# Attention and two expert layers on one core: new load order at the start, and the first batch's units in five stretches

## The chip, the core and the metric

The program runs on one core of a Trainium2 chip. The time is the device time of one execution in microseconds (us). Five engines with an instruction queue each take part: PE (TensorE, matmuls), DVE (VectorE), ACT (ScalarE), POOL (GpSimd) and SP (SyncE, which here issues DMAs). Every queue runs in order: an instruction that waits holds all that stand behind it.

## What is computed

```python
def _attn_ref(q, k, v, p):                 # q, k, v: [4, 8, 576, 64], p: [4, 8, 32, 64]
    p_packed = sm_attn(p, k, v)            # softmax attention of the 32 pack rows on the 576 keys
    return sm_attn(q, p_packed, p_packed)  # the 576 queries on the 32 packed rows
...
x = attn_out.transpose(0, 2, 1, 3).reshape(2304, 512)
h = x @ w_in;  y = (h * tanh(softplus(h))) @ w_out        # w_in [512, 2048], w_out [2048, 512], "mish"
h = y @ w_in2; out = where(h > 0, h, exp(min(h, 0)) - 1) @ w_out2
```

The weights come as float64 and are read as pairs of 32-bit words.

## The kernel before

**Weights.** A weight tile of 128 rows is loaded raw (`load_raw`, line 127, on SP's queue) and decoded to float32 by `decode`: `s0` on ACT (line 162 in the start-up form `exps=True`, line 164 later), then on DVE `s1` (169), `s2` (177, only without `exps`) and `s3` (182). A tile of w_out (named `w1o0` to `w1o15`, of which `w1o4` holds the rows of unit index 4) is then split into a high and a low part, on ACT (204) and DVE (210). A tile of w_in (`w1i r c`: four row blocks r of each of four column groups c) stays whole; `fold` (line 523) multiplies column group c by the packed rows of a batch and gives `G[b, c]`, split by ACT (204) and DVE (210).

**Units.** The first layer is done in 128 units: batch b, token half e (288 tokens), 128 columns kk of the hidden layer. `gemm1` (563 to 565, 6 matmuls) makes the first product from `G[b, kk // 4]`, `mish` (572 to 574, ACT, ACT, DVE) the activation, and `gemm2` (591 to 593, 12 matmuls), two units later, adds the unit into an accumulator. The accumulators of one token half fill both buffers of `ps_a`: when the units pass to the other half, the next `gemm2` waits until `y` has been copied out (line 275, half on ACT and half on DVE, or added on DVE at 603 where the half has been there before). `order1` gives the order of the units. For batch 0 it is four stretches of eight units: half 0 with kk 0 to 7, half 1 with kk 0 to 7, half 0 with kk 8 to 15, half 1 with kk 8 to 15. So a new column group of w_in is needed at units 0, 4, 16 and 20.

**Order of the rest.** `startup()` writes out by hand the attention of batch 0 and the decode of the first eight weight tiles; its PE, DVE, ACT and SP work stands in that order. `mixture1()` then walks over the units and puts between them, by due times, the decode of the other 24 tiles (`DEC1`), the folds of batch 0 (`F0`), the attention and the folds of batch 1 (`ATT1`, `FOLDOFF`), the reloads of decoded w_in tiles (`RELOFF`) and, from unit 34, the second layer's weights. Tile's scheduler orders what comes from there; where `keep_in_program_order` is called, the instruction keeps its place among those marked like it. ACT needs another function table for the exponentials of an attention than for Mish: each change is an `ACT_TABLE_LOAD`.

**Loads at the start.** On SP: two small parts of p for batch 0, the four k tiles, two raw tiles, q, eight raw tiles. On ACT: two small parts of p, then v. On POOL: the p of the other batches. The DMAs of SP and ACT share eight semaphores, so the ninth waits for the first to land. PE runs `WARM` matmuls on the identity matrix before its first real work.

Of the kernel before, what the change touches and what calls it, by code (L numbers as in the profile page):

```python
# [18 lines left out]
    DEC1=[9, 37],  # L19
    F0=[3, 12, 17],  # L20
# [6 lines left out]
    RELOFF=-5,  # L27
    NU=28,
    EVA='va',
    WARM=16,  # L30
    YL=[12, 13, 14],
# [10 lines left out]
def kernel(  # L42
# [81 lines left out]
    def load_raw(name, r, c):  # L124
# [5 lines left out]
        if name[1] == "2":  # L130
            tc.keep_in_program_order(ins)
# [108 lines left out]
    def load_heads(src, dst, b, g, nm, eng):  # L240
# [9 lines left out]
        elif nm == "k" or b == 0:  # L250

            t = home([128, S // 32, 32], F32, f"{nm}{b}_{g}")
            eng.dma_start(
                out=t.rearrange("p c d -> p (c d)"),
                in_=src[b, 2 * g:2 * g + 2].rearrange("h (t j) d -> (h t) (j d)", t=64),
            )
        else:
# [24 lines left out]
    def transpose_heads(src, dst, b, g, nm):  # L282
        def blocks32():
            o = small([128, 2, HALF], F32, f"{nm}{b}_{g}")
            nc.vector.transpose(
                out=o.rearrange("p e s -> p (e s)"), in_=src.pop((b, g)).rearrange("p c d -> p (c d)")
            )
            dst[b, g] = o

        return [blocks32]  # L290
# [259 lines left out]
    order1 = [(e, h * NK // 2 + i) for h in range(2) for e in range(2) for i in range(NK // 2)]  # L550
# [210 lines left out]
    DEC1 = P["DEC1"]  # L761

    def startup():
        pr = [slot([128, n * H // 2, D], F32, f"pr{n}") for n in (1, B - 1)]
        ps_ = p.rearrange("b (g s) n d -> s n (b g) d", s=2)
        for x, (a, n) in enumerate(((0, H // 2), (H // 2, (B - 1) * H // 2))):
            for s in range(2):
                for th in range(2):
                    r = 64 * s + 32 * th
                    eng = nc.gpsimd if x else (nc.sync, nc.scalar)[s]  # L770
                    eng.dma_start(out=pr[x][r:r + 32], in_=ps_[s][:, a:a + n, :])
# [9 lines left out]
        nc.scalar.preload_act_table_set("exp_and_others")  # L781
# [9 lines left out]
        dec = [decode(*w1dec.popleft(), exps=True) for _ in range(8)]  # L791
# [4 lines left out]
        def turn_p(x):  # L796
# [7 lines left out]
            hk[0][0], hk[1][0], hk[2][0], hk[3][0], sc[0][0], sc[1][0], sc[0][1], sc[1][1], *parts(0, 0), sc[0][2],  # L804
            a1t0[0], a1t0[1], a1t1[0], a1t1[1], *parts(1, 0), pk[0][0], hq[0][0], hq[1][0], sc[1][2], *parts(0, 1, 3, 4),
            pk[1][0], pk[0][1], hq[2][0], hq[3][0], pk[0][2], pk[1][1], *parts(2, 0), *parts(3, 0), *parts(1, 1, 3, 4),
# [160 lines left out]
```

## Time and profile before

| what | value |
|---|---|
| three runs, median (lowest to highest) | 819.1 us (817.96 to 820.22) |
| profiled execution, its span | 817.5 us |
| PE busy | 776.2 us (95%) |
| DVE busy, ACT busy | 439.6 us (54%), 341.2 us (42%) |
| chain that ended last | PE 85%, DVE 7%, DMA 4%, ACT 3% |

No time of the profiled execution itself is given beside its span; the lowest run lies 0.5 us above the span and the median 1.6 us. The page's strip of 40 slices shows PE at nine tenths or more from the eighth slice on, and in the first seven slices (some 143 us) less; there DVE stands at eight to nine tenths in most slices, and the granted PE clock is below full in five of the first six. The granted clock has two levels, 2.4 GHz (1.00) and 1.2 GHz (0.50); a value between is a mean over a stretch.

### The profile page before, as it was taken

How to read it: one execution, taken by the hardware profiler on the slowest of the kernel's cores; microseconds unless marked ns; L12 is line 12 of the kernel's file. 1: busy time of each engine (PE TensorE's matmuls, PEld its weight loads, DVE VectorE, ACT ScalarE, POOL GpSimd, SP SyncE). 2: the span in 40 equal slices, each digit the busy share in tenths (PEclk: the TensorE clock that was granted, in tenths of full speed). 3: DMA queues.
4: the chain of work that ended last, by engine and by line, in shares of the span. 5: the costliest groups of instructions: out<-in, count | busy, mean ns of one | idle time of the engine just before them, and what ended most of it. 6: DMA issues, size and time to landing. Idle time of an engine off the chain costs nothing.

```text
span 817.5 us, 13068 instructions
## 1 busy us (share of the span) xinstructions
PE 776.2 (95%) x5212; PEld 669.6 (82%) x5212; DVE 439.6 (54%) x845; ACT 341.2 (42%) x672; POOL 25.0 (3%) x50
## 2 busy tenths in 40 slices
PE   6468879999999999999999999999999999999997
PEld 5147769889888998999998888888888888888886
DVE  3998886955687448573427743422352334332342
ACT  2347744666475746564434432312231223221322
POOL 1000000000001010000000000000000000000000
PEclk8787979999999999999999999999999999999999
DMA  9962973376656774440682311200030001000000
GB/s 250 411 242 90 326 175 147 124 235 133 215 195 221 191 207 164 150 134 30 227 292 79 102 52 35 68 1 1 1 90 1 1 1 51 14 1 0 35 18 26
DMA packets 67837, 96.80 MB, mean 118 GB/s; under 512 B 34624, under 2 KB 43328, under 8 KB 67776
## 3 DMA queue, kind: packets, MB, share of 16 engines
q1 hardware_dynamic: 61408, 77.02, 29.8%
q0 software_dynamic: 4928, 17.70, 5.5%
q10 hardware_dynamic: 1440, 1.25, 0.7%
q8 instruction: 41, 0.67, 0.3%
q14 instruction: 20, 0.16, 0.1%
HBM read 73.92 MB, written 22.02 MB: 117 GB/s over the span
## 4 chain that ended last, share of the span: by engine, by line
PE 85%; DVE 7%; DMA 4%; ACT 3%; issue 1%; ACTq 0%; SPq 0%; DVEq 0%
PE h L654 8%; PE h L655 8%; PE h L653 8%; PE o L676 8%; PE o L677 8%; PE o L678 8%; PE acc L592 7%; PE acc L591 7%; PE acc L593 7%; PE h L563 4%; PE h L564 4%; PE h L565 4%; PE pm L523 1%; DMA raw_w1o<-in_moe_w_out_dram 1%; DMA v<-in_v_dram 1%
## 5 line engine op out<-in xcount | busy, mean ns | idle before, releaser
L592 PE MATMUL acc<-gl,w1oh 128*128 128x288 f32 x512 | 152.5, 300 | 1.6 <-DVE gl L574 1.4
L593 PE MATMUL acc<-gh,w1ol 128*128 128x288 f32 x512 | 151.7, 299 | 0.0
L591 PE MATMUL acc<-gh,w1oh 128*128 128x288 f32 x512 | 148.9, 298 | 2.6 <-DVE y L275 2.6
L654 PE MATMUL h<-yl,w2ih 128*128 128x512 f32 (+1 forms) x320 | 117.7, 368 | 0.0
L655 PE MATMUL h<-yh,w2il 128*128 128x512 f32 (+1 forms) x320 | 117.5, 368 | 0.0
L653 PE MATMUL h<-yh,w2ih 128*128 128x512 f32 (+1 forms) x320 | 116.6, 368 | 0.0
L676 PE MATMUL o<-w2oh,gh 128*128 128x512 f32 x288 | 112.4, 390 | 1.1 <-ACT ob L273 0.7
L677 PE MATMUL o<-w2ol,gh 128*128 128x512 f32 x288 | 112.2, 390 | 0.0
L657 ACT ACTIVATE t<-h 128x512 f32<-128x512 f32 (+1 forms) x80 | 42.8, 553 | 165.5 <-PE h L655 151.0
L658 DVE TENSOR_SCALAR t<-t 128x512 f32<-128x512 f32 (+1 forms) x80 | 31.7, 399 | 142.5 <-ACT t L657 141.7
L678 PE MATMUL o<-w2oh,gl 128*128 128x512 f32 x288 | 108.3, 389 | 0.0
L592 PEld LDWEIGHTS acc<-gl,w1oh 128*128 128x128 f32 x512 | 97.4, 190 | 9.1 <-DVE gl L574 5.0
L591 PEld LDWEIGHTS acc<-gh,w1oh 128*128 128x128 f32 x512 | 96.3, 191 | 7.4 <-DVE y L275 4.6
L593 PEld LDWEIGHTS acc<-gh,w1ol 128*128 128x128 f32 x512 | 97.2, 190 | 3.9 <-issue 3.6
L574 DVE TENSOR_TENSOR gl<-t,gh 128x288 fp32r<-128x288 f32 x128 | 57.7, 453 | 78.2 <-ACT gh L573 77.6
L563 PE MATMUL h<-a2h,gh 128*128 128x288 f32 x256 | 78.4, 309 | 9.7 <-ACT a2h L204 6.0
L572 ACT ACTIVATE t<-h 128x288 f32<-128x288 f32 x128 | 52.1, 408 | 84.1 <-PE h L565 81.8
L564 PE MATMUL h<-a2l,gh 128*128 128x288 f32 x256 | 77.5, 303 | 3.0 <-DVE a2l L208 3.0
L204 ACT ACTIVATE gh<-t 128x512 fp32r<-128x512 f32 (+1 forms) x80 | 46.6, 588 | 78.6 <-DVE t L659 49.1
L565 PE MATMUL h<-a2h,gl 128*128 128x288 f32 x256 | 76.9, 302 | 0.0
L208 DVE TENSOR_TENSOR gl<-t,gh 128x512 fp32r<-128x512 f32 (+1 forms) x80 | 50.2, 637 | 41.0 <-ACT gh L204 39.5
L653 PEld LDWEIGHTS h<-yh,w2ih 128*128 128x128 f32 x320 | 60.3, 188 | 10.3
(107 smaller groups left out, 1098.7 us busy)
## 6 DMA issues: line engine op xcount, KB each, us to landing
w1r<-w_dr SPq DMA_DIRECT2D x24, 512.0 KB, 6.0
raw_w1i<-in_moe_w_in_dram SPq DMA_DIRECT2D x16, 512.0 KB, 8.9
raw_w1o<-in_moe_w_out_dram SPq DMA_DIRECT2D x16, 512.0 KB, 8.2
raw_w2i<-in_moe_w_in_dram SPq DMA_DIRECT2D x16, 512.0 KB, 4.3
raw_w2o<-in_moe_w_out_dram SPq DMA_DIRECT2D x16, 512.0 KB, 3.8
k<-in_k_dram SPq DMA_DIRECT2D x16, 288.0 KB, 7.2
y_dr<-y POOLq DMA_DIRECT2D x16, 288.0 KB, 3.8
w_dr<-w1v POOLq DMA_DIRECT2D x8, 512.0 KB, 6.1
```

The costliest lines, as they stand in the source:

```text
L563: nc.tensor.matmul(out=hp, lhsT=wh, rhs=xh, start=(kt == 0), stop=False)
L564: nc.tensor.matmul(out=hp, lhsT=wh, rhs=xl, start=False, stop=False)
L565: nc.tensor.matmul(out=hp, lhsT=wl, rhs=xh, start=False, stop=(kt == 1))
L591: nc.tensor.matmul(out=o, lhsT=wh[:, cs], rhs=gh, start=first, stop=False)
L592: nc.tensor.matmul(out=o, lhsT=wh[:, cs], rhs=gl, start=False, stop=False)
L593: nc.tensor.matmul(out=o, lhsT=wl[:, cs], rhs=gh, start=False, stop=last)
L653: nc.tensor.matmul(out=hp, lhsT=wh, rhs=xh, start=(i == 0), stop=False)
L654: nc.tensor.matmul(out=hp, lhsT=wh, rhs=xl, start=False, stop=False)
L655: nc.tensor.matmul(out=hp, lhsT=wl, rhs=xh, start=False, stop=(i == 3))
L676: nc.tensor.matmul(out=o, lhsT=gh[:, ts], rhs=wh, start=(kk == 0), stop=False)
L677: nc.tensor.matmul(out=o, lhsT=gh[:, ts], rhs=wl, start=False, stop=False)
L678: nc.tensor.matmul(out=o, lhsT=gl[:, ts], rhs=wh, start=False, stop=(kk == NK - 1))
```

## The change

At the start, the four k tiles are issued by SP and ACT in turn, v goes from ACT's queue to SP's, behind k; the raw tiles are interleaved with q, and the p of batches 1 to 3 goes from POOL's queue to SP's, behind the first eight raw tiles. `EXPS` = 12 tiles instead of 8 are decoded in `startup()` in its form without `s2`; four of them are column group 1 of w_in. The w1 loads, the k loads of batch 1 and their transposes keep their program order. The units of batch 0 come in five stretches: half 0 with kk 0 to 3, half 1 with 0 to 7, half 0 with 4 to 11, half 1 with 8 to 15, half 0 with 12 to 15. A new column group is needed at units 0, 8, 16 and 24, and the accumulators pass to the other half at units 4, 12, 20, 28 and 32. The due times `F0`, `DEC1` and `RELOFF` move with it, and the y tiles of batch 0 lie in the pool `up`.

```diff
-    DEC1=[9, 37],
-    F0=[3, 12, 17],
+    DEC1=[10, 32],
+    F0=[6, 14, 20],
...
-    RELOFF=-5,
+    RELOFF=(-2, -5),
+    EXPS=12,
...
-        if name[1] == "2":
-            tc.keep_in_program_order(ins)
+        tc.keep_in_program_order(ins)
...
+            if b == 1:
+                tc.keep_in_program_order(ins)
...
-    order1 = [(e, h * NK // 2 + i) for h in range(2) for e in range(2) for i in range(NK // 2)]
+    order1 = [(e, kk) for e, a, n in ((0, 0, 1), (1, 0, 2), (0, 1, 2), (1, 2, 2), (0, 3, 1)) for kk in range(4 * a, 4 * (a + n))]
...
-        first = kk == 0 or (blk < 2 and kk == NK // 2)
-        last = kk == NK - 1 or (blk < 2 and kk == NK // 2 - 1)
+        first = n == 0 or order1[n - 1][0] != blk
+        last = n + 1 == len(order1) or order1[n + 1][0] != blk
...
-                    ysum[blk, d] = small([128, 2, HALF], F32, f"y{blk}_{d}")
+                    ysum[blk, d] = (small if blk > 1 else slot)([128, 2, HALF], F32, f"y{blk}_{d}")
...
+        load_p(0, (nc.sync, nc.scalar))
...
-            load_heads(k, kt_in, 0, g, "k", nc.sync)
-        for kt in range(2):
-            load_vt(0, kt, nc.scalar)
+            load_heads(k, kt_in, 0, g, "k", (nc.sync, nc.scalar)[g % 2])
         nc.scalar.preload_act_table_set("exp_and_others")
-        load_w1(2)
         for kt in range(2):
+            load_vt(0, kt)
+        for kt in range(2):
+            load_w1(1)
             load_kt(q, qt_in, 0, kt, "q")
         load_w1(6)
-        load_w1(LEAD)
+        load_p(1, (nc.sync, nc.sync))
+        load_w1(EXPS - 8 + LEAD)
...
-        dec = [decode(*w1dec.popleft(), exps=True) for _ in range(8)]
+        dec = [decode(*w1dec.popleft(), exps=True) for _ in range(EXPS)]
...
-                at.setdefault(i0 + NK + 4 * c + P['RELOFF'], []).append(lambda c=c: reload_w1i(c))
+                at.setdefault(i0 + NK + 4 * c + P['RELOFF'][b > 1], []).append(lambda c=c: reload_w1i(c))
```

The hand-written list in `startup()` changes too: the first raw tile is decoded after the transposes of the first attention, not before, and `s0` of the four tiles of column group 1 stands at the list's end, ahead of the units.

On ACT, where the units begin (h1 is a unit's first product, t1 its activation; a2h0 belongs to the attention of batch 0; w1oh0 is the high part of w_out's first rows), before:

```order
L162 ACTIVATE raw_w1o3_0_191<-raw_w1o3_0_191 128x512
L204 ACTIVATE a2h0_431<-a2t0_1_445 128x576
L572 ACT_TABLE_LOAD
L572 ACTIVATE t1_489<-h1_482 128x288
L204 ACTIVATE w1oh0_0_199<-dec_201 128x512
```

and now:

```order
L162 ACTIVATE raw_w1o3_0_187<-raw_w1o3_0_187 128x512
L204 ACTIVATE a2h0_441<-a2t0_1_455 128x576
L162 ACTIVATE raw_w1i0_1_193<-raw_w1i0_1_193 128x512
L162 ACTIVATE raw_w1i1_1_195<-raw_w1i1_1_195 128x512
L162 ACTIVATE raw_w1i2_1_197<-raw_w1i2_1_197 128x512
L162 ACTIVATE raw_w1i3_1_199<-raw_w1i3_1_199 128x512
L204 ACTIVATE w1oh0_0_207<-dec_209 128x512
L576 ACT_TABLE_LOAD
L576 ACTIVATE t1_499<-h1_492 128x288
```

The four `s0` of column group 1 and one split now stand ahead of the table load and of the first Mish.

On DVE, from the last decode step of column group 1 (`w1v1_2` from `raw_w1i3_1`, which releases the second fold) to the copies of `y`, now:

```order
L182 SCALAR_TENSOR_TENSOR w1v1_2_216<-raw_w1i3_1_199,w1v1_2_216 128x512
L806 STREAM_TRANSPOSE pT3_98<-pr3_118 128x768
L177 SCALAR_TENSOR_TENSOR dec_602<-raw_w1o6_0_522,dec_602 128x512
L169 TENSOR_SCALAR dec_638<-raw_w1o7_0_564 128x512
L182 SCALAR_TENSOR_TENSOR dec_602<-raw_w1o6_0_522,dec_602 128x512
L177 SCALAR_TENSOR_TENSOR dec_638<-raw_w1o7_0_564,dec_638 128x512
L182 SCALAR_TENSOR_TENSOR dec_638<-raw_w1o7_0_564,dec_638 128x512
L210 SCALAR_TENSOR_TENSOR w1ol6_0_601<-dec_602,w1oh6_0_600 128x512
L277 COPY y0_0_670<-acc0_546 128x288
L277 COPY y0_1_673<-acc1_547 128x288
```

Before, behind the same step:

```order
L182 SCALAR_TENSOR_TENSOR w1v1_2_501<-raw_w1i3_1_470,w1v1_2_501 128x512
L182 SCALAR_TENSOR_TENSOR dec_570<-raw_w1o4_0_499,dec_570 128x512
L210 SCALAR_TENSOR_TENSOR w1ol4_0_569<-dec_570,w1oh4_0_568 128x512
L210 SCALAR_TENSOR_TENSOR gl0_1_603<-pm_557,gh0_1_602 128x512 x2
L169 TENSOR_SCALAR dec_610<-raw_w1o5_0_519 128x512
```

Before, the fold's own splits (`gl0_1`) followed it closely; now seven instructions stand between the step that releases the fold and the first copy of `y0`, which the fifth unit's second product waits for. On PE the fold stood behind the first products of units 0 to 3 and now stands behind those of units 0 to 7; the second products of units 4 to 6 follow it.

On ACT, at the change to the third stretch (e1_1_1 are the exponentials of batch 1; the copies of y1 free the accumulators for unit 12), now:

```order
L577 ACTIVATE gh1_1014<-t1_1013 128x288
L329 ACT_TABLE_LOAD
L329 ACTIVATE e1_1_1_955,sm_952<-pm_923,sm_952 128x2x5x32
L329 ACTIVATE e1_1_1_955,sm_952<-pm_923,sm_952 128x2x4x32
L164 ACTIVATE raw_w1o10_0_850<-raw_w1o10_0_850 128x512
L164 ACTIVATE raw_w1o11_0_889<-raw_w1o11_0_889 128x512
L576 ACT_TABLE_LOAD
L576 ACTIVATE t1_1073<-h1_1066 128x288
L576 ACTIVATE t1_1113<-h1_1106 128x288
L577 ACTIVATE gh1_1074<-t1_1073 128x288
L204 ACTIVATE w1oh10_0_960<-dec_962 128x512
L275 ACTIVATE y1_0_1031<-acc0_707 128x288
```

and before, at its change to the second stretch:

```order
L572 ACTIVATE t1_828<-h1_821 128x288
L573 ACTIVATE gh1_829<-t1_828 128x288
L273 ACTIVATE y0_0_846<-acc0_539 128x288
L273 ACTIVATE y0_1_849<-acc1_540 128x288
L164 ACTIVATE raw_w1o8_0_759<-raw_w1o8_0_759 128x512
L572 ACTIVATE t1_873<-h1_866 128x288
L573 ACTIVATE gh1_874<-t1_873 128x288
L204 ACTIVATE w1oh8_0_857<-dec_859 128x512
L325 ACT_TABLE_LOAD
```

Before, the copies stood ahead of the table load of those exponentials; now the copies of this change stand behind both table loads, two decode steps and a split.

## Rows read from the trace of the kernel before

**Rows 1.** Windows: PE, PEld, DVE, ACT, POOL busy, granted clock, DMA, GB/s:

```profile
36.00:44.00 8.00, 4.89 (x18) 4.19 (x19) 7.75 (x15) 4.81 (x10) 0.00 (x0) 0.53 1.03 409
53.00:59.20 6.20, 0.15 (x2) 0.00 (x0) 6.20 (x13) 0.08 (x1) 0.53 (x1) 0.84 0.57 182
59.20:71.00 11.80, 11.00 (x76) 7.58 (x77) 9.12 (x17) 6.36 (x13) 0.53 (x1) 0.50 0.53 179
71.00:97.00 26.00, 22.74 (x196) 20.16 (x195) 19.74 (x43) 19.82 (x39) 1.06 (x2) 1.00 0.56 194
97.00:109.00 12.00, 10.97 (x116) 10.48 (x116) 11.21 (x24) 10.19 (x24) 0.53 (x1) 1.00 0.55 203
109.00:117.20 8.20, 4.10 (x68) 1.36 (x66) 6.16 (x14) 1.54 (x4) 0.53 (x1) 0.67 1.01 275
117.20:122.20 5.00, 5.00 (x21) 5.00 (x22) 4.25 (x8) 1.89 (x4) 0.00 (x0) 0.51 0.78 130
122.20:160.20 38.00, 37.92 (x320) 34.44 (x319) 27.82 (x55) 19.39 (x38) 1.09 (x2) 1.00 0.40 140
```

**Rows 2.** Windows of L565 alone (PE, PEld busy, clock, DMA, GB/s):

```profile
36.00:97.00 61.00, 10.02 (x30) 7.02 (x30) 0.83 0.62 223
```

**Rows 3.** Windows of L593 alone, the same columns:

```profile
36.00:97.00 61.00, 15.33 (x52) 10.02 (x52) 0.83 0.62 223
```

**Rows 4.** Timeline, start of program: start, length, instruction, [idle before <-releaser]:

```profile
4.40 6.23 PE L776 MATMUL warm<-ident 128*128 128x128 f32 x32 [4.40 <-POOL ident masks.py:199]
...
11.64 0.78 DVE L285 STREAM_TRANSPOSE kT<-k 128x576 f32<-128x576 f32 x1 [2.17 <-DMA k<-in_k_dram]
...
12.48 3.08 PE L306 MATMUL pm<-kT,pT 32*32 32x288 f32 x64 [1.84 <-DVE kT L285]
...
19.34 1.53 DVE L285 STREAM_TRANSPOSE qT<-q 128x576 f32<-128x576 f32 x2 [0.51 <-DMA q<-in_q_dram]
...
25.36 0.43 DVE L275 COPY pt<-pm 64x256 f32<-64x256 f32 x1
```

**Rows 5.** Timeline, DVE in the decode of the first units:

```profile
46.12 1.19 DVE L574 TENSOR_TENSOR gl<-t,gh 128x288 fp32r<-128x288 f32 x3
...
54.41 0.75 DVE L169 TENSOR_SCALAR w1v<-raw_w1i 128x512 int32<-128x512 int32 x2
...
55.09 0.68 DVE L182 SCALAR_TENSOR_TENSOR w1v<-raw_w1i,w1v 128x512 int32<-128x512 int32 x1
...
55.69 0.68 DVE L177 SCALAR_TENSOR_TENSOR w1v<-raw_w1i,w1v 128x512 int32<-128x512 int32 x1
```

**Rows 6.** Timeline, ACT and DVE where the units begin:

```profile
34.16 1.21 ACT L162 ACTIVATE raw_w1o<-raw_w1o 128x512 f32<-128x512 f32 x2
...
39.98 1.28 ACT L572 ACT_TABLE_LOAD   x1
...
40.67 0.42 DVE L169 TENSOR_SCALAR dec<-raw_w1o 128x512 int32<-128x512 int32 x1
```

**Rows 7.** Timeline, PE: the second fold:

```profile
59.26 1.96 PE L523 MATMUL pm<-w1v,pt 64*32 64x512 f32 x16 [6.11 <-DVE w1v L182]
```

**Rows 8.** Chain of waits, ACT: start, length, what:

```profile
74.33 1.07 ACT e L325 x4
```

**Rows 9.** Timeline, PE after the first table switch:

```profile
77.76 0.40 PE L563 MATMUL h<-a2h,gh 128*128 128x288 f32 x1 [1.48 <-ACT t L572]
```

**Rows 10.** Timeline, PE at the full clock:

```profile
100.00 0.30 PE L593 MATMUL acc<-gh,w1ol 128*128 128x288 f32 x1
...
100.14 0.29 PE L592 MATMUL acc<-gl,w1oh 128*128 128x288 f32 x1
```

**Rows 11.** Timeline, SP, ACT and PE around 116 us:

```profile
109.46 10.57 SPq L262 DMA_DIRECT2D q<-in_q_dram  x12
...
115.66 0.65 ACT L164 ACTIVATE raw_w1o<-raw_w1o 128x512 f32<-128x512 f32 x1 [6.84 <-DMA raw_w1o<-in_moe_w_out_dram]
...
117.16 0.61 PE L591 MATMUL acc<-gh,w1oh 128*128 128x288 f32 x1 [2.07 <-DVE y L275]
```

More of the change, by code (lines that the diff above doesn't have):

```diff
@@ L252, in load_heads @@
             t = home([128, S // 32, 32], F32, f"{nm}{b}_{g}")
-            eng.dma_start(
+            ins = eng.dma_start(
                 out=t.rearrange("p c d -> p (c d)"),
@@ L284, in blocks32 @@
             o = small([128, 2, HALF], F32, f"{nm}{b}_{g}")
-            nc.vector.transpose(
+            ins = nc.vector.transpose(
                 out=o.rearrange("p e s -> p (e s)"), in_=src.pop((b, g)).rearrange("p c d -> p (c d)")
             )
+            if b == 1 and nm == "kT":
+                tc.keep_in_program_order(ins)
             dst[b, g] = o
@@ L761 @@
     DEC1 = P["DEC1"]
+    EXPS = P["EXPS"]
     def startup():
@@ L765, in startup, with load_p @@
         ps_ = p.rearrange("b (g s) n d -> s n (b g) d", s=2)
-        for x, (a, n) in enumerate(((0, H // 2), (H // 2, (B - 1) * H // 2))):
+        def load_p(x, engs):
+            a, n = ((0, H // 2), (H // 2, (B - 1) * H // 2))[x]
             for s in range(2):
@@ L769, in startup @@
                     r = 64 * s + 32 * th
-                    eng = nc.gpsimd if x else (nc.sync, nc.scalar)[s]
-                    eng.dma_start(out=pr[x][r:r + 32], in_=ps_[s][:, a:a + n, :])
+                    engs[s].dma_start(out=pr[x][r:r + 32], in_=ps_[s][:, a:a + n, :])
+        load_p(0, (nc.sync, nc.scalar))
         make_identity(nc, ident)
@@ L777, in startup @@
         for g in range(4):
-            load_heads(k, kt_in, 0, g, "k", nc.sync)
+            load_heads(k, kt_in, 0, g, "k", (nc.sync, nc.scalar)[g % 2])
+        nc.scalar.preload_act_table_set("exp_and_others")
         for kt in range(2):
-            load_vt(0, kt, nc.scalar)
-        nc.scalar.preload_act_table_set("exp_and_others")
-        load_w1(2)
+            load_vt(0, kt)
         for kt in range(2):
+            load_w1(1)
             load_kt(q, qt_in, 0, kt, "q")
         load_w1(6)
-        load_w1(LEAD)
+        load_p(1, (nc.sync, nc.sync))
+        load_w1(EXPS - 8 + LEAD)
         at = attention_steps(0)
@@ L803, in startup @@
         order = [
-            hk[0][0], hk[1][0], hk[2][0], hk[3][0], sc[0][0], sc[1][0], sc[0][1], sc[1][1], *parts(0, 0), sc[0][2],
-            a1t0[0], a1t0[1], a1t1[0], a1t1[1], *parts(1, 0), pk[0][0], hq[0][0], hq[1][0], sc[1][2], *parts(0, 1, 3, 4),
-            pk[1][0], pk[0][1], hq[2][0], hq[3][0], pk[0][2], pk[1][1], *parts(2, 0), *parts(3, 0), *parts(1, 1, 3, 4),
-            pk[1][2], s2[0], *parts(2, 1, 3, 4), *parts(3, 1, 3, 4), s2[1], s2[2], f0[0], s2[3], s2[4], f0[1],
-            *parts(4, 0), *parts(5, 0), s2[5], f0[2], *parts(6, 0), *parts(7, 0), s2[6], s2[7],
+            hk[0][0], hk[1][0], hk[2][0], hk[3][0], sc[0][0], sc[1][0], sc[0][1], sc[1][1], sc[0][2],
+            a1t0[0], a1t0[1], a1t1[0], a1t1[1], *parts(0, 0), pk[0][0], hq[0][0], hq[1][0], sc[1][2], *parts(0, 1, 3, 4),
+            pk[1][0], pk[0][1], *parts(1, 0), pk[0][2], pk[1][1], hq[2][0], hq[3][0], *parts(1, 1, 3, 4), *parts(2, 0),
+            pk[1][2], s2[0], *parts(3, 0), *parts(2, 1, 3, 4), *parts(3, 1, 3, 4), s2[1], s2[2], f0[0], s2[3], s2[4],
+            f0[1], *parts(4, 0), *parts(5, 0), s2[5], f0[2], *parts(6, 0), *parts(7, 0), s2[6], s2[7],
+            *[f for n in range(8, EXPS) for f in parts(n, 0)],
             *parts(4, 1, 3, 4), *parts(5, 1, 3, 4), *parts(4, 5), *parts(6, 1, 3, 4), *parts(5, 5), *parts(7, 1, 3, 4),
-            *parts(6, 5), *parts(7, 5), lambda: turn_p(1),
+            *parts(6, 5), *parts(7, 5), *[f for n in range(8, EXPS) for f in parts(n, 1, 3, 4)], lambda: turn_p(1),
         ]
```

## The prediction

> **What bounds the kernel now.** I read the strip of slices first: behind some 122 us PE is full and its clock is at the upper level, and nothing there is touched but orders that have slack. So I looked at the windows of the stage before it [rows 1]. From 122.2 to 160.2 PE is busy 37.92 of 38.0 us; before that it has two holes, and a half-rate stretch (granted clock 0.50, that is 1.2 GHz) behind each. The first hole is 53.0 to 59.2: PE had run everything it could, and waits 6.11 us for DVE, which decodes column group 1 [rows 7]; the clock is then 0.50 until 71. The second is around 109 to 117.2: a raw w_out tile stands on SP behind twelve of the sixteen loads of batch 1's q, ACT waits 6.84 us for it, and the copies of y stand behind that on ACT, so PE waits too [rows 11]; the clock is 0.67 there and 0.51 until 122.2. DVE is busy all of 53.0 to 59.2 and 9.12 of 11.8 us in the next window [rows 1]: in the first hole DVE is the bound, in the second a DMA queue.
>
> **A worksheet.** I walk the new order of the three engines with durations of these rows. DVE, back to back: a decode step 169 is 0.34 (two in 0.68, 54.41 to 55.09), steps 177 and 182 and the split 210 are 0.60 (55.09 to 55.69), a unit's low part 574 is 0.40 (three in 1.19) [rows 5]. ACT: a step 162 or 164 is 0.61, a table load 1.28 [rows 6], the exponentials of one half 1.07 [rows 8]; Mish and its copies I take at 0.40 to 0.45, as the DVE operation of the same size. PE: a matmul of a unit every 0.14 us at full clock [rows 10], more exactly 0.132, twice that at half; a unit is 0.8 us of first and 1.6 us of second product. The fold is 1.96 us at half rate [rows 7], 1.0 at full. As a test, before's own 36 DVE instructions from the start of the units at 40.67 [rows 6] to the fold's release at 59.2 add up to 18.5 us that way.
>
> **Start-up.** The last k tile holds its transpose until 11.64, and PE's scores start at 12.48 [rows 4]. With k alone on two queues and v and the large p behind it, k can land four us earlier; but PE's warm-up ends at 4.40 + 6.23 = 10.63 [rows 4], so the scores move by 1.8 us only. Behind them q no longer lands last (19.34 waited for q, [rows 4]); then the hand-written list waits for itself: the copy of the packed rows pt now comes before two transposes of q, which used to fill the wait for PE. From 20.0 I count pv 0.2, PE's turns 1.0, pt 0.4, pv 0.2, two transposes 1.5, a decode 1.0, so that the second pt begins near 24.3 instead of 25.36 [rows 4]. **Term: -1.05 us**; units start on DVE at 39.6. The bounds are 0 (the wait for PE costs what the start gained) and -1.8. The large p on SP costs nothing: its transpose is now used 20 us behind its landing.
>
> **First hole.** From 39.6 DVE has 37 instructions up to the step that releases the second fold: eleven of 0.34, eighteen of 0.60, seven of 0.40 and one transpose of 0.7, together 18.0. Four decodes are without step 177, which takes 2.4 us out, but seven low parts instead of four stand there and two w_out tiles have come ahead. Added is a wait: ACT does four steps 162 (2.4 us) and a split before the table load, so the first Mish ends near 44 and its copy 1.7 us behind the place where DVE needs it; dependent pairs add 0.5. The fold is released at 59.8, against 59.26: no earlier. But PE has by then done eight first products instead of four, until about 54.7, and waits 5.1 instead of 6.11. Behind the fold (to 61.8) it stands before unit 4's second product, which needs the copies of y; they lie behind 4.4 us of DVE work and the ACT split that waits for it, near 64.8. That is a new wait of 3.0 us. Then the half rate goes on. How long is not in the order; the rows give from about 4 us of busy time (36.0 to 44.0 has 0.53 and PE resumed near 40) over 5.0 (117.2 to 122.2) to 11.8 (59.2 to 71.0) [rows 1]. I take 5.5, near the middle row, which costs 2.75 us.
>
> **Second stretch to third.** From 64.8 PE has no wait but short ones until unit 12 (the first table switch, which cost it 1.48 us before [rows 9], now falls where a score and two second products are still queued): 96 matmuls of second and 48 of first products are 19.0, two scores 2.2, turns and fold 1.7, half rate 2.75, together 25.7, so 90.5. There the accumulators change hands. DVE's and ACT's copies stand behind the block that the order shows on ACT: it begins near 88.2 (behind the scores of the second half and two w_out tiles) and takes 1.28 + 1.07 + 1.2 + 1.28 + 0.85 + 0.45 + 0.6 = 6.7 before the copies, and DVE's copy comes 2.1 later than ACT's turn, since three decode steps stand ahead of it. PE resumes at 97.0: **a new hole of 6.5 us**, with half rate behind it again.
>
> **At 97 us the two stand equal.** Before has done 15 units' first products (30 rows of line 565, two each, [rows 2]) and 13 units' second (52 rows of line 593, four each, [rows 3]); the new order has 16 and 12 and one block of transposes more. That is 0.8 + 0.65 - 1.6, nothing. Everything gained until there is given back at the change of stretch.
>
> **From 97 on.** Before needs 63.2 us to 160.2, where unit 31's second product ends. Of that 9.7 are lost: 1.0 in the window to 109, 4.1 idle to 117.2 and half of the other 4.1 for the clock, 2.45 to 122.2, 0.1 behind [rows 1]. In the new order q's loads go out in two parts from about 94 on, the raw tiles 12 and 13 ahead of or between them, and both are needed only near 109 to 112: no DMA ends last. That leaves 53.5 of work. The losses that come in its place are the half rate behind 97 (2.75), the wait of group 3's split for the last w_out tiles (0.7), the change at unit 20, whose adds find DVE free to within 1 us, and the low part of unit 31 behind batch 2's transposes (1.2): some 5.7. 53.5 + 5.7 = 59.2, so 156.2 against 160.2: **-4.0 us**, with the start-up term inside it. Behind this point the matmuls and their order are before's, at 100% of PE.
>
> The Trainium skill, "TensorE: Matmul & The Clock Gate", Part 1, says that "the default state is throttled, and activity releases the throttle". By that rule the clock would come back soon behind each gap, as in the first of the three rows, and the sum would be 3.5 us lower than mine. The trace agrees only in part: in 59.2 to 71.0 PE is busy 11.0 of 11.8 us and the clock stays at 0.50 [rows 1].
>
> **The rivals.** (a) The clock returns within 4 us behind both gaps, and DVE's short waits hide: twice (2.75 - 2.0), and 2 us of the 3.0 and 1.2 us waits; -4.0 - 1.5 - 2.0 = -7.5, so 810.0 of span and 811.6 of median. For it: the 36 to 44 row; against it: the 59.2 to 71 row. (b) No difference: the new holes cost what the old did. DVE's rows over the 32 units lose 2.4 us (four steps 177) and gain four adds of 0.4; were DVE the bound throughout, this is all that changes, -0.8, a median of 818.3. For it: DVE busy 19.74 of 26 and 11.21 of 12 [rows 1]; against it: PE was the late one from 117 on. (c) Slower: q's transposes of batch 1 now stand on DVE ahead of the adds that free the accumulators at unit 20, and q's last loads wait for the transposes and products of batch 1's attention, as their sixteen did before over ten us and more [rows 11]. My walk has the last land near 116 and the adds at 120.8, when PE comes. From 4 to 5 us later on it is PE's wait; landing 10 us late costs 5.5 and a half-rate stretch, 2.75 to 5.9, together 8.3 to 11.4, and -4.0 turns to +4.3 to +7.4, a median of 823.4 to 826.5. It breaks even near 6 us late. For it: before had its worst stall in this very queue; against it: eight of the sixteen go out without a wait for PE. (d) The change doesn't do what it says: k isn't first in effect, since the warm-up ends at 10.63; that costs the 1.05 and is within (b).
>
> **How the numbers follow.** The span of the profiled execution is 817.5; -4.0 gives 813.5, and the median of the runs lies 1.6 above the span, so 815.1. Chances: my forecast (-2.5 to -6.5) 0.46, (a) 0.17, (b) 0.2, (c) 0.17. A difference under 0.3%, 2.5 us, is about what a measurement of this kernel can't tell from none. Faster by more: 0.46 + 0.16 = 0.62; within: 0.21; slower: 0.17. The range leaves out the late end of (c) and little else: down to 819.1 - 11 = 808, which is (a) with the rule's 3.5 us on both stretches, and up to 819.1 + 2.4 = 821.5, which is (b) with both stretches at half rate as long as the longest row, or (c) with q some 8 us late.
>
> **What would show it.** Right: scores on PE start near 10.7; DVE's first step of the units near 39.6; the second fold near 60 behind eight first products; a PE gap before unit 4's second product near 62 to 65 and a gap of 5 to 8 us ending near 97 that the copies of y end; no DMA wait of ACT near 109 to 116; unit 31's last product near 156. Wrong: a fold before 57 (then DVE waits less for ACT than I count, and several us more are won), no gap near 90 to 97, or one near 120 that q's transposes or the adds end. The clock's half-rate stretches are the least known term: 1.75 to 5.9 us each.

## The result

The changed kernel takes 810.2 us (median of 4 runs, 809.9 to 811.3) against 819.6 for the kernel before: a ratio of 0.9893, 95% interval 0.9879 to 0.9907, or 9.3 us less. Timed once more it was 810.8 against 821.2, ratio 0.9881 (0.9865 to 0.9898). The forecast was 815.1, with a range of 808.0 to 821.5: the direction was right, and the 4.0 us forecast are less than half of the 9.3 measured. The profiled execution has a span of 808.7 us, 8.8 less than before; the sum had promised 4.0.

To compare it with the walk of the prediction I cut the span at five marks, each of them the start (for unit 31 the end) of a row of the timeline. "After, again" is the second profiled execution of the same kernel (run 12).

| mark (us) | before | predicted | after | after, again |
|---|---|---|---|---|
| units begin on DVE | 40.7 | 39.6 | 37.5 | 39.7 |
| unit 4's second product | 68.9 | 64.8 | 61.8 | 64.4 |
| unit 12's second product | 95.2 | 97.0 | 93.7 | 96.6 |
| unit 31's second product ends | 160.0 | 156.2 | 152.8 | 154.3 |
| end of the span | 817.5 | 813.5 | 808.7 | 810.2 |

The marks cut the two kernels' holes otherwise. Now the accumulators change hands for the first two times at units 4 and 12, so each hole ends at a mark. Before, it was at units 8 and 16: the second hole ends at unit 16's second product (117.2 us), behind the mark of unit 12.

The windows of the changed kernel between these marks answer to [rows 1]. Columns: length, busy time of PE, PEld, DVE, ACT and POOL with counts, granted clock, DMA share, GB/s.

```profile
37.49:61.82 24.33, 16.14 (x109) 14.67 (x108) 22.90 (x47) 16.25 (x35) 1.07 (x2) 0.78 0.78 280
61.82:65.40 3.58, 3.58 (x15) 3.58 (x16) 3.54 (x7) 1.51 (x3) 0.00 (x0) 0.50 0.46 154
65.40:85.50 20.10, 20.00 (x195) 18.16 (x194) 15.74 (x33) 13.03 (x27) 1.06 (x2) 1.00 0.70 234
85.50:93.69 8.19, 2.98 (x23) 0.78 (x22) 6.39 (x17) 8.09 (x17) 0.00 (x0) 0.74 0.08 22
93.69:99.50 5.81, 5.81 (x24) 5.81 (x25) 5.37 (x10) 1.43 (x3) 0.08 (x1) 0.50 0.94 241
99.50:152.80 53.30, 52.26 (x496) 46.43 (x495) 43.65 (x89) 28.88 (x61) 2.08 (x4) 1.00 0.56 178
```

The shape is the foreseen one: DVE busy 22.9 of 24.3 us up to the first copies, half rate, 20 us of dense PE work, a hole in which ACT is busy 8.09 of 8.19 us, half rate again, and then 1.0 us of idle time in 53. The list of what PE waited for up to 170 us (total, times, longest), here some of its rows, has the waits of [rows 7, 9, 11] in their new places:

```profile
PE acc L595 <- DVE y L277: 4.8, 2, 3.6
...
PE h L567 <- ACT t L576: 2.8, 3, 1.8
PE pm L527 <- DVE w1v L182: 2.8, 1, 2.8
PE pm L527 <- DVE a1t L277: 2.2, 1, 2.2
```

The second fold waits 2.8 us for DVE's step 182 instead of 6.11, and the copies of y now cost 4.8 us in two waits, 3.6 ahead of unit 4 and 1.2 ahead of unit 12. The start, in the timeline, answers to [rows 4]; of the warm-up x32 counts records, and each of the 16 products leaves two:

```profile
1.36 6.72 PE L784 MATMUL warm<-ident 128*128 128x128 f32 x32 [1.36 <-POOL ident masks.py:199]
...
7.28 1.44 DVE L287 STREAM_TRANSPOSE kT<-k 128x576 f32<-128x576 f32 x2 [0.22 <-DMA k<-in_k_dram]
...
8.78 1.95 PE L310 MATMUL pm<-kT,pT 32*32 32x288 f32 x64 [0.70 <-DVE kT L287]
...
37.49 0.42 DVE L169 TENSOR_SCALAR dec<-raw_w1o 128x512 int32<-128x512 int32 x1
```

PE's warm-up starts at 1.36 us, not at 4.40: the identity that it waits for stood on POOL behind the four loads of the large P, and these have left POOL. The scores then wait for k alone. The hole at the change to the third stretch is the one that was announced, here on ACT and DVE; DVE's copies come last, 1.6 us behind ACT's, and end it:

```profile
85.14 1.28 ACT L329 ACT_TABLE_LOAD   x1
...
88.64 1.28 ACT L576 ACT_TABLE_LOAD   x1
...
91.56 0.69 ACT L275 ACTIVATE y<-acc 128x288 f32<-128x288 f32 x2
...
93.19 0.81 DVE L277 COPY y<-acc 128x288 f32<-128x288 f32 x2
```

### The profile page after: what moved, and what is told of

It reads as the page before. It is cut to its first block, busy times and chain, and to the rows that moved or that the text cites. A ratio compares the mean times of both kernels' runs of the same rounds, so it can differ in the third digit from the quotient of the medians.

```text
span 808.7 us, 13064 instructions
## 1 busy us (share of the span) xinstructions
PE 774.3 (96%) x5212; PEld 669.9 (83%) x5212; DVE 437.6 (54%) x845; ACT 340.5 (42%) x672; POOL 22.5 (3%) x46
## 4 chain that ended last, share of the span: by engine, by line
PE 90%; DVE 4%; ACT 3%; DMA 2%; issue 1%; SPq 0%; DVEq 0%; ACTq 0%
PE acc L595 8%; PE acc L596 8%; PE acc L597 8%; PE h L659 8%; PE h L658 8%; PE h L657 8%; PE o L680 8%; PE o L681 8%; PE o L682 8%; PE h L567 4%; PE h L568 4%; PE h L569 4%; PE pm L527 2%; DMA k<-in_k_dram 1%; PE pm L310 1%; DMA v<-in_v_dram 1%
## 5 line engine op out<-in xcount | busy, mean ns | idle before, releaser
L659 PEld LDWEIGHTS h<-yh,w2il 128*128 128x128 f32 x320 | 60.3, 188 | 10.3
```

The lines of the kernel that those rows point to most:

```text
L659: nc.tensor.matmul(out=hp, lhsT=wl, rhs=xh, start=False, stop=(i == 3))
```

## The experiments

Times are medians; ratios are to runs of the kernel before on the same chip. My theory after the result was that the start had been worth more than the 1.05 us I gave it; the rival, that the new order of units had.

**1. P's loads on POOL ahead of the identity again**

```diff
         load_p(0, (nc.sync, nc.scalar))
+        load_p(1, (nc.gpsimd, nc.gpsimd))
         make_identity(nc, ident)
...
-        load_p(1, (nc.sync, nc.sync))
```

> The changed kernel with one thing undone: the four loads of the large P go out on POOL ahead of the identity again, as in the kernel before; k, v and q keep their new queues. In the changed kernel PE's warm-up starts at 1.36 us and ends at 8.08, the scores start at 8.78 and DVE's unit phase at 37.49. Theory A (the warm-up starts with the identity, which stood behind these loads on POOL, and what the start gains is carried to the end, because DVE has no slack between the start and the second column group): warm-up 4.4 to 10.6, scores near 10.7, unit phase near 39.5, time 2.0 us longer, near 812.2. Theory B (the start's gain is lost again in the waits ahead of the third stretch; what was won comes from the new order of units): the scores move, the time stays within 0.7 us of 810.2. Theory C (P's traffic matters as well, it lands with k): scores after 11.5, time 3 us or more longer.

815.3 us, ratio 0.9937 (0.9912 to 0.9961): 5 us back, more than any theory said. Its scores start at 10.70 us, right behind the warm-up, and the units at 40.58:

```profile
4.40 6.37 PE L785 MATMUL warm<-ident 128*128 128x128 f32 x32 [4.40 <-POOL ident masks.py:199]
...
10.70 1.70 PE L310 MATMUL pm<-kT,pT 32*32 32x288 f32 x56
...
40.58 0.42 DVE L169 TENSOR_SCALAR dec<-raw_w1o 128x512 int32<-128x512 int32 x1
```

But the edit also changed the order that the planner (Tile's scheduler) gave to what stands behind the start: 43 rows of PE, some 10 of DVE and 8 of ACT stand elsewhere. From the first copies to unit 12 this kernel takes 34.21 us against 31.87, a stretch that no load of the start touches. So this run does not give the price of P's place; run 9 does it better.

**2. A longer warm-up**

```diff
-    WARM=16,
+    WARM=22,
```

> The changed kernel with 22 warm-up products instead of 16, so that PE's warm-up ends near 10.6 instead of 8.08 us, as I had assumed of the changed kernel; every load stays as it is. Theory A (the end of the warm-up alone sets the scores once k is first, and its end is carried on): scores near 10.7, unit phase 2 us later, time near 812.2. Theory B (lost again later): within 0.7 us of 810.2. If it differs from the run with P on POOL by over 1 us, P's traffic counts by itself.

812.1 us, 0.9902 (0.9887 to 0.9917), the same as the changed kernel. It didn't do what it was for: the products took half the time from some 6 us on, so that 22 of them ended at 8.7, and the scores waited for k as before. The planner moved some 14 rows of PE here too, without a visible cost.

```profile
1.36 7.37 PE L784 MATMUL warm<-ident 128*128 128x128 f32 x44 [1.36 <-POOL ident masks.py:199]
9.50 0.85 PE L310 MATMUL pm<-kT,pT 32*32 32x288 f32 x17 [0.78 <-DVE kT L287]
```

**3. All loads of the start as before.** The edit puts the old block of loads in the place of the new one (P on POOL, k on SP alone, v on ACT, two raw tiles ahead of q).

> The changed kernel with all loads of the start as in the kernel before: P on POOL ahead of the identity, k on SP alone, v on ACT, two raw tiles, then q. Units in the new order, twelve tiles by the short decode. Theory A: scores near 12.5, unit phase near 40.5, time 3.0 to 3.5 us longer than the changed kernel, near 813.5. Theory B: within 1 us of 810.2. Above 815: the old loads also delay w tiles that the new order needs early.

815.1 us, 0.9939 (0.9924 to 0.9954). Scores at 11.85, units at 41.47, 4.0 us later than in the first profile of the changed kernel and 1.8 later than in the second; the time to unit 31's end from there is 116.2 against 115.3 and 114.7. The start is most of what came back, and the planner has moved here exactly as in run 1.

**4. The order of units, fold places, decode pace and number of short decodes of before, the loads new**

```diff
-    order1 = [(e, kk) for e, a, n in ((0, 0, 1), (1, 0, 2), (0, 1, 2), (1, 2, 2), (0, 3, 1)) for kk in range(4 * a, 4 * (a + n))]
+    order1 = [(e, h * NK // 2 + i) for h in range(2) for e in range(2) for i in range(NK // 2)]
...
-    DEC1=[10, 32],
-    F0=[6, 14, 20],
-    EXPS=12,
+    DEC1=[9, 37],
+    F0=[3, 12, 17],
+    EXPS=8,
```

> The changed kernel with the unit order of the kernel before (four stretches of eight), its fold units, its decode pace and eight tiles by the short decode; the loads of the start and the kept order of raw tiles and k on SP stay new. Theory A (start and stretches add up; start 3.2 us, stretches some 6): near 816.4. Theory D (the kept order of loads on SP, not the stretches, took the wait behind q's loads away, and that wait is most of the rest): near 811 to 812, with no wait of ACT for a raw tile near 106 to 116. Theory E (without the early start the old order would have its DVE-bound hole anyway, which swallows the start): near 819.

813.7 us, 0.9925 (0.9909 to 0.9942), between theory A and theory D; ACT waits for no raw tile from 100 to 118 us, as D has it. With the old units, the rest of the change alone is worth 6.0 of the 9 us, and the five stretches add about 3. Against before its parts are: start -3.0, from there to unit 4's second product -4.4, to unit 12 -1.6, to unit 31 +3.1, rest -0.4. Its windows between the marks:

```profile
37.71:61.54 23.83, 18.02 (x110) 15.35 (x109) 21.25 (x41) 13.78 (x28) 1.06 (x2) 0.83 0.73 277
61.54:86.32 24.78, 23.22 (x226) 20.30 (x225) 22.68 (x51) 19.90 (x42) 1.06 (x2) 1.00 0.76 239
86.32:154.15 67.83, 61.11 (x541) 52.75 (x540) 55.02 (x111) 37.29 (x77) 2.16 (x4) 0.92 0.54 161
```

Where the 4.4 us went, with the same order of units, is seen for the larger part in DVE's groups behind the start of the units. Before, up to the second fold (busy, mean ns, idle before), and then the changed kernel, up to the copies of y:

```profile
L285 DVE STREAM_TRANSPOSE kT<-k 128x576 f32<-128x576 f32 x4 | 3.0, 764 | 0.0
```

```profile
L287 DVE STREAM_TRANSPOSE kT<-k 128x576 f32<-128x576 f32 x1 | 0.8, 761 | 0.0
```

Before, all four transposes of batch 1's k stood on DVE between the start of the units and the step that releases the fold, 3.0 us on the engine that ended the first hole. Kept in program order, one stands there now and none in run 4, where the fold comes 16.0 us behind the start of the units instead of 18.6. The other 1.8 us lie behind the fold: PE waited 2.3 us for it instead of 6.11, and the clock stayed at 1.00 up to unit 4's second product, where before it was 0.50. My count had the transpose in its 37 instructions, but as one row among many. No run undoes the kept order of k by itself, nor `RELOFF`, nor the pool of the y tiles, so what each of them is worth is not shown.

**5. Fourteen products of the identity in the first gap**

```diff
             if i < NA:
                 mish(i)
+            if i in FILL:
+                fill(FILL[i])
```

where `fill` is so many `matmul(out=f[:, 0:128], lhsT=ident, rhs=ident)` into a tile of the `h` pool, and FILL is {7: 14}.

> The changed kernel with 14 extra products of the identity on PE (0.42 us each, their result is not used) between unit 7's first product and the second fold; nothing else differs on any engine. In the changed kernel PE idles most of 54.5 to 61.8 us, the clock falls to 0.50 near 59.3 and is back at 65.4, so 61.8 to 65.4 runs at half rate. Theory A (this half rate costs PE 1.8 us, and what is won there is kept): clock 1.00 through the gap, unit 4's second product still near 61.8, time 1.5 to 1.8 us less, near 808.5. Theory B (the next gap, 86 to 93.7, is ended by ACT and DVE and swallows it): time within 0.5 us of 810.2. Theory C (the fold is late behind the fill and its splits with it): 1 us or more longer.

810.1 us, 0.9884 (0.9865 to 0.9903): no difference. The products took 0.235 us each instead of 0.42, PE idled 3.25 us behind them, and the clock was down when it resumed:

```profile
60.05:63.30 3.25, 0.00 (x0) 0.00 (x0) 3.21 (x7) 2.28 (x6) 0.00 (x0) 1.00 0.99 312
63.30:66.30 3.00, 2.96 (x13) 2.96 (x14) 3.00 (x6) 0.93 (x3) 0.00 (x0) 0.54 0.40 124
```

**6. The kernel before, with the raw tiles kept in order on SP**

```diff
-        if name[1] == "2":
-            tc.keep_in_program_order(ins)
+        tc.keep_in_program_order(ins)
```

> The kernel before with one edit: the raw tiles of the first layer's weights keep their program order on SP. In the kernel before, raw w_out tile 12 stands behind twelve of q's sixteen loads, ACT waits 6.84 us for it, PE idles 4.1 us around 109 to 117 and runs at half rate for 5 us more. Theory A (the order on this queue alone makes that hole): ACT's wait gone, hole gone, 4 to 6.5 us less than 819.6, near 814. Theory B (the attention of batch 1 makes PE, DVE and ACT wait for each other there anyway, as the run with the old stretches still shows 5 us of PE's idle time in 98 to 109): 1 to 3 us less, near 817.5. Theory C: q comes late instead; no gain or slower.

819.0 us, 0.9995 (0.9981 to 1.0009). The wait of ACT for the raw tile is gone; ACT's list for 100 to 122 us has only engines in it, and PE's hole is still there, 3.6 us of idle time where [rows 1] has 4.1, and half rate behind it:

```profile
ACT y L272 <- PE pm L376: 2.7, 1, 2.7
ACT gh L203 <- DVE gl L209: 2.3, 1, 2.3
```

```profile
109.00:117.00 8.00, 4.44 (x103) 2.59 (x103) 7.61 (x17) 2.32 (x6) 0.53 (x1) 0.90 0.88 219
117.00:122.00 5.00, 5.00 (x23) 5.00 (x22) 2.69 (x5) 1.16 (x2) 0.00 (x0) 0.50 1.00 185
```

Without a wait of 6.84 us the time is the same; the interval leaves a gain of some 1.6 us at most. PE waits for the later of the copies of y. ACT's come 4.0 us earlier than before (112.20 instead of 116.22), but DVE's only 1.0, behind decode steps and a transpose of q that keep DVE busy 7.61 of 8.00 us. In run 6 and before:

```profile
115.65 0.82 DVE L274 COPY y<-acc 128x288 f32<-128x288 f32 x2
```

```profile
116.64 0.82 DVE L275 COPY y<-acc 128x288 f32<-128x288 f32 x2 [1.44 <-ACT y L273]
```

The planner moved some 20 rows of PE here as well, so the price of the wait alone is not isolated.

**7. Eight short decodes instead of twelve**

```diff
-    EXPS=12,
+    EXPS=8,
```

> The changed kernel with eight tiles by the short decode instead of twelve: four more steps 177 of 0.60 us on DVE ahead of the second fold, 2.4 us. Theory A (DVE is the bound from the unit phase at 37.5 to the copies at 61.8, and what it loses goes to the end): the copies near 64.2 and the time 2.0 to 2.4 us longer, near 812.4. Theory B (swallowed in the gap of 86 to 93.7): within 0.7 us of 810.2.

815.8 us, 0.9953 (0.9935 to 0.9971): 5 us longer, so theory B falls, and theory A's 2.0 to 2.4 us are less than half of it. From the start of the units to unit 4's second product it takes 26.27 us, 1.6 to 1.9 more than the changed kernel, near the 2.4 of the four steps. To unit 12 another 1.9 follow (33.77 against 31.87), but the planner moved there too, as in run 1, and I can't split that.

**8. Batch 1's attention from unit 5**

```diff
-    ATT1=4,
+    ATT1=5,
```

> The changed kernel with batch 1's attention due from unit 5 instead of unit 4, which puts the copies of y at unit 12 ahead of ACT's second table load instead of behind it. Theory A (the gap of 86 to 93.7, 5.2 us of PE's waits and 5.8 us of half rate behind it, is made by the copies' place behind ACT's block of two table loads): waits under 2 us there, little half rate, 3 to 6 us less, near 806. Theory B (the exponentials then come later and PE waits for the transposes or the fold instead): within 1.5 us of 810.2. Theory C (batch 1's attention is late at unit 32): slower by 1 us or more.

810.9 us, 0.9891 (0.9869 to 0.9914): no difference. The copies at unit 12 do come earlier, and the stretch between the two sets of copies falls from 31.87 to 27.40 us; but the one before it grows from 24.33 to 26.27 and the one behind it from 59.11 to 62.93.

```profile
63.73:91.13 27.40, 24.09 (x209) 22.24 (x209) 22.52 (x46) 17.16 (x36) 1.06 (x2) 0.91 0.61 198
91.13:154.06 62.93, 59.89 (x539) 52.01 (x540) 52.02 (x107) 34.97 (x74) 2.15 (x4) 0.97 0.56 165
```

The copies can thus come earlier without a gain; what was won in this stretch was lost on either side. The planner moved many rows here, some 130 of PE, so the run doesn't show which of them cost it.

**9. P's loads on POOL, written behind the identity**

```diff
         make_identity(nc, ident)
+        load_p(1, (nc.gpsimd, nc.gpsimd))
...
-        load_p(1, (nc.sync, nc.sync))
```

> The changed kernel with the large P's four loads on POOL again, but behind the identity instead of ahead of it: PE's warm-up starts at 1.36 us as in the changed kernel, P's traffic is early as in the kernel before. The orders of PE, DVE and ACT are word for word those of the changed kernel. The run with P ahead of the identity was 5.0 us longer. Theory A (the late warm-up made that): scores between 8.8 and 10.1, where the last k tile lets them start, time near 810.5. Theory C (P's traffic made it, by q and the first w tiles landing later): DVE's wait for q stays, the unit phase starts near 39.5 and the time is 3 us or more longer than 810.2.

811.5 us, 0.9883 (0.9862 to 0.9904); the changed kernel on the same chip 810.8, 0.9881. One premise was off: the identity is two instructions on POOL, three of P's issues went between them, and the warm-up started at 3.79.

```profile
3.79 5.19 PE L785 MATMUL warm<-ident 128*128 128x128 f32 x32 [3.79 <-POOL ident masks.py:199]
...
9.26 0.78 DVE L287 STREAM_TRANSPOSE kT<-k 128x576 f32<-128x576 f32 x1 [0.46 <-DMA k<-in_k_dram]
...
39.65 0.42 DVE L169 TENSOR_SCALAR dec<-raw_w1o 128x512 int32<-128x512 int32 x1
```

The warm-up ended at 8.98 us, ahead of the last k tile's transpose (10.04), so the scores waited for k; in run 1 it had ended at 10.77, 0.8 us behind that transpose (9.94). So this run leaves open what a later warm-up costs. It shows that P's traffic on POOL's queue costs nothing that can be measured where PE, DVE and ACT keep the changed kernel's order. Run 1's profile is 4.1 us longer than this one: 0.9 at the start of the units, 0.8 to unit 4's second product, 2.2 from there to unit 12, 0.2 behind. The larger part lies where the two kernels differ in the planner's order alone. The same stretch from unit 4 to unit 12 takes 33.1 to 34.2 us in runs 1, 3, 7 and 11, where the planner moved rows, and 31.2 to 32.2 in the five executions with the changed kernel's order (the kernel twice, runs 5, 9 and 10); run 2, with 14 rows moved, takes 31.9.

**10. Twenty-two products in the first gap.** Run 5 with FILL {7: 22}.

> The run with 14 extra products again, now with 22: they took 0.235 us each, not 0.42, so that PE still idled 3.3 us before unit 4's second product and the clock fell there all the same. 22 of them end some 1 us ahead of that product; nothing else differs on any engine. Theory A (half rate of 3 to 3.6 us behind this gap costs 1.5 to 1.8 us and is kept): clock 1.00 through 54 to 70, and the stretch from the copies of y to unit 8's second product 1.5 to 1.8 us shorter (it was 10.47 in the changed kernel); time 1.5 less, near 808.7. Theory B (the gap of 86 to 94, which ACT and DVE end, takes it back): that stretch is shorter, the copies of y at unit 12 are where they were against the start of the units, time within 0.7 of 810.2.

809.0 us, 0.9859 (0.9841 to 0.9878), the shortest of all, though its interval overlaps the changed kernel's. PE and the clock through the gap:

```profile
54.53 5.07 PE L557 MATMUL fill<-ident 128*128 128x128 f32 x44
59.53 1.09 PE L529 MATMUL pm<-w1v,pt 64*32 64x512 f32 x16
61.93 0.40 PE L602 MATMUL acc<-gh,w1oh 128*128 128x288 f32 x1 [1.31 <-DVE y L279]
```

```profile
61.90:64.90 3.00, 2.97 (x22) 2.97 (x23) 3.00 (x6) 0.93 (x3) 0.00 (x0) 1.00 0.23 70
...
61.93:93.09 31.16, 25.73 (x230) 21.24 (x230) 25.73 (x54) 22.49 (x45) 1.06 (x2) 0.90 0.53 169
```

The clock stays at 1.00, and unit 8's second product comes 8.9 us behind unit 4's instead of 10.5 (10.8 in run 12): 1.6 to 1.9 us, as theory A has it. At unit 12's second product only 0.7 to 1.1 of it is left (31.16 against 31.87 and 32.22). And the 22 products held the fold back: it comes 22.4 us behind the start of the units instead of 19.7, and unit 4's second product 24.8 instead of 24.3 and 24.7. Counted from the start of the units, unit 12 is reached after 55.9 us, against 56.2 and 56.9: 0.3 to 1.0 us is left, so theory B holds for half of it or more, and the shorter time is not shown to come from the clock.

**11. P's large transpose behind the first copies.** The edit takes `turn_p(1)` from the end of the list of the start and issues it, in program order, at unit 8.

> The changed kernel with the transpose of the large P (0.96 us on DVE, between the second fold's release and the first copies of y) moved behind those copies. Theory A (DVE has no slack up to the first copies): copies and unit 4's second product 0.9 us earlier against the start of the units, time 0.9 to 2 us less, between 808.2 and 809.3. Theory B (PE's gain there is taken back in the gap of 86 to 94): within 0.7 us of 810.2.

813.1 us, 0.9906 (0.9889 to 0.9923), 2 us longer than the changed kernel by the medians, though the intervals just touch. Unit 4's second product comes 23.50 us behind the start of the units instead of 24.33, near the 0.9 expected; to unit 12 it then takes 33.82 instead of 31.87. DVE was the bound there, and yet the gain was lost and more: the planner moved 23 rows of PE and 10 of DVE.

```profile
37.38:60.88 23.50, 16.10 (x110) 14.64 (x109) 22.07 (x46) 16.27 (x35) 1.33 (x2) 0.79 0.78 277
60.88:94.70 33.82, 26.95 (x229) 22.89 (x230) 26.58 (x55) 22.27 (x45) 1.06 (x2) 0.85 0.55 179
```

**12. The changed kernel again**

> The changed kernel once more, as the one to compare with on the same chip, and to see how far the start of the scores (8.77 us in its first profile, 8.9 to 10.1 in kernels with the same loads) varies from run to run. Theory: the last k tile's landing varies by up to 1.4 us and the start of the units with it; time 809.8 to 811.5.

810.8 us, 0.9881 (0.9865 to 0.9898). The last k tile is transposed at 9.34 us instead of 8.72, and the units start at 39.67, within 0.1 us of the prediction:

```profile
8.56 0.78 DVE L287 STREAM_TRANSPOSE kT<-k 128x576 f32<-128x576 f32 x1 [0.17 <-DMA k<-in_k_dram]
...
39.67 0.42 DVE L169 TENSOR_SCALAR dec<-raw_w1o 128x512 int32<-128x512 int32 x1
```

```profile
39.67:64.35 24.68, 16.61 (x109) 15.14 (x109) 23.13 (x47) 16.32 (x35) 1.07 (x2) 0.78 0.73 259
64.35:96.57 32.22, 26.89 (x229) 22.84 (x230) 25.71 (x54) 22.59 (x45) 1.07 (x2) 0.87 0.54 166
96.57:154.32 57.75, 56.70 (x518) 50.88 (x519) 49.01 (x99) 30.31 (x64) 2.15 (x4) 0.97 0.63 188
```

## Why the prediction was right, and what it missed

The span fell 4.8 us further than the sum in the first profile and 3.3 us further in the second. By the marks of the table:

- **Start-up (predicted -1.05, bounds 0 to -1.8): mis-sized, and the bound was wrong.** The step that failed is "PE's warm-up ends at 4.40 + 6.23 = 10.63". I took that row of [rows 4] for a constant, though it names the identity on POOL as what PE waited for, and though I had P leave POOL in the same paragraph: each queue that an instruction leaves has others behind it. In seven executions with the new loads (both of the changed kernel, runs 2, 5, 8, 10 and 11) the units start between 37.2 and 39.7, on average 38.2; in three with the old loads (before, runs 3 and 6) between 40.7 and 41.5, on average 41.2. That is -3.0 on average, with single pairs from -1.0 to -4.3. In the seven the scores start between 8.8 and 10.1, on average 9.3, that is 1.4 ahead of the 10.7 forecast, and the units on average 1.4 ahead of 39.6; single executions don't pair up that well (run 12: scores 1.3 ahead, units not at all). What the scores wait for in these seven is the last k tile, whose transpose ended at 12.4 us before. How much of it is P's leaving POOL is not settled: with P ahead of the identity (run 1) the warm-up ended 0.8 us behind k, and run 9's start, 39.65, lies inside the new kernel's own spread.
- **Units to the first copies (25.2 predicted): 24.3 and 24.7.** The fold comes 19.7 and 20.0 us behind the start of the units (20.2 predicted), behind eight first products, and the new wait before unit 4 is 3.6 us (3.0). PE's wait before the fold was 2.8 instead of 5.1, which changes nothing, since the copies end the stretch. Run 7 adds 1.6 to 1.9 of the 2.4 us that four steps of DVE should cost, and run 11 takes off 0.8 of 0.96: DVE is the bound here.
- **To unit 12 (32.2 predicted): 31.9 and 32.2.** The hole is there, ended by DVE's copies, 1.6 us behind those that stand on ACT behind its two table loads; PE's waits in it are 1.8 + 2.2 + 1.2 = 5.2 us, where I had 6.5 and had put the transposes and the fold ahead of it instead of inside.
- **To unit 31 (59.2 predicted): 59.1 and 57.8.** Here two errors met. The losses are 2.9 for the half rate and 1.0 of idle time, 3.9 instead of 5.7; the work without them is 59.1 - 3.9 = 55.2, not 53.5. That 59.1 agrees with 59.2 is luck. Of the 1.7 us some 0.7 is a reading of [rows 1]: I put all 4.1 us of PE's busy time in 109 to 117.2 at half rate, but the clock fell at 111.85 and only 2.7 of them came after that, so before loses 9.0 there and not 9.7. Another 0.5 is the four matmuls of the next point; the rest is open.
- **The rest (657.3 predicted, as before): 655.9 twice.** "Behind this point the matmuls and their order are before's" was wrong by 1.4 to 1.6 us. Unit 31 ends with 34 units' first products done instead of 33 1/3, which is 4 matmuls, some 0.5 us, and before has another 0.5 us of idle time from 160.0 to 163.0 (PE busy 2.52 of 3.00), where after has none; over the whole rest PE's idle time differs by 0.2 us (5.3 against 5.1). The other half was not traced.

Against the kernel before, the start gave 3.2 us in the first profile and 1.0 in the second (1.05 predicted), the stretch from there to unit 31's end 4.0 and 4.7 (2.9), the rest 1.6 in both (nothing). So in the first profile 2.1 us of the 4.8 are the start, 0.9 the first stretch, 0.3 and 0.1 the next two and 1.4 the rest; in the second the start is on the forecast, and the whole miss is 0.5 + 1.4 + 1.4 us of smaller terms on the same side. With a start that varies by 2.5 us between executions, neither the one nor the other is typical.

**The half rate**, 5.5 us behind each gap, was 3.6 and 5.8 in the first profile, 4.4 and 2.9 in the second: a price of 1.4 to 2.9 us each, where the prediction had 1.75 to 5.9. What it is worth is less than the rows say: run 10 took the first one away, won 1.6 to 1.9 us on the spot and kept at most 1.1 of it to unit 12. The Trainium skill, "TensorE: Matmul & The Clock Gate", Part 1, states that activity releases the throttle. The trace agrees behind the first gap (3.6 and 4.4 us) better than my middle row did; behind the second the clock stayed down for 5.8 us of unbroken work in one execution and 2.9 in the other.

**Two sums of the prediction don't come out.** The 3.5 us that an early return of the clock was to save aren't in the rows: the first row, about 4 us of busy time, saves twice 0.75, as rival (a) has it. And the low end of the range takes these 3.5 off (a), which has 1.5 of them in it already: -4.0 - 3.5 - 2.0 is -9.5, or 809.6, not 808. The high end, 821.5, is (b) with one long stretch, not with both, which would be 824.6. The measured 810.2 lies inside either way.

**The reading of the second hole was wrong.** I called a DMA queue its bound, from [rows 11]. Run 6 took that wait away and 0.7 us, not distinguishable from none, came of it. ACT indeed has no DMA wait in the changed kernel near 109 to 116, as I said, but that is not where the gain of the third stretch comes from. With the old order of units and the new loads (run 4) the stretch from unit 12 to unit 31's end is 67.8 us, longer than before's 64.8; with the new order 59.1. The new order pays 5.5 us to unit 12 and gets 5.6 back here against before; against run 4 it pays 7.1 and gets 8.7. Much of that is the place of the mark: the second hole ends at unit 12 now and at unit 16 in the other two. From the start of the units to unit 31's end, with every hole inside, it is 115.3 and 114.7 us now, 116.4 in run 4 and 119.3 before.

**The rivals.** (a), 811.6, came nearest in time, and of its two causes one held: short waits hide (1.0 us after unit 12), while the clock came back within 4 us behind the first gap only (in the second profile behind the second only). It would have needed the start as well. (c) did not occur: unit 20's second product waits for nothing. (b)'s remark that the new holes cost what the old did doesn't hold: from the start of the units to unit 31's end PE is idle 14.5 us in both profiles, before 16.8, and its busy time falls from 102.5 to 100.8 and 100.2 us with four matmuls more in it.

## What to carry to other kernels

The wait that ends last in a hole is not its price: of the waits and half-rate stretches that were removed or moved here, two gave back no time that can be measured (runs 6 and 8) and one at most a part (run 10). In run 6 another engine's work ended right behind it; sum each engine's work between two marks instead. When a transfer leaves a queue, look for what stood behind it there, down to a constant that only a warm-up needs. And where a scheduler orders the code, an edit in one place moves instructions in others: compare the orders before a run is read as the price of the edit, and compare stages from a common mark, since the start alone varied by 2.5 us.

## What was not expected of the hardware

The same loads land at different times: the last k tile's transpose ended between 8.7 and 10.1 us in kernels with identical loads, and the units began up to 2.5 us apart.

A product of the identity took 0.42 us on average in the warm-up (6.72 us for 16) and 0.23 in the middle of the kernel (5.07 for 22, run 10). The windows give a granted clock of 1.00 for both, here for the warm-up of the changed kernel:

```profile
4.00:6.00 2.00, 2.00 (x11) 2.00 (x10) 0.55 (x2) 0.00 (x0) 0.00 (x0) 1.00 1.03 385
```

But the trace's first entry of the granted clock is at 7.4 us in this execution, and ahead of it the 1.00 is no measurement. The products themselves show both rates: in run 2, 11 records fall into the 2.00 us from 2.00 to 4.00, and 16 into the 1.50 us from 7.00 to 8.50. The warm-up thus begins at half rate, and when the rate rises differs: the same 16 products took 6.72 us in the changed kernel and 5.65 in run 10.

The clock went down behind 3.25 us of idle time (run 5) and stayed up behind 1.1 (run 10), in kernels that differ in eight products only; in run 4, which has another order of units, it stayed up behind a wait of 2.3 us. Behind the gap at unit 12 the changed kernel ran at half rate for 5.8 us in one execution; in the other a window of 5.63 us from the same product had a mean of 0.74, about half of it:

```profile
96.57:102.20 5.63, 5.63 (x33) 5.63 (x34) 5.56 (x11) 1.87 (x4) 0.00 (x0) 0.74 0.97 248
```
